# Sliding-window attention and a two-layer MLP on one core: batch 0's shifted values copied block by block, and block 0's first product taken input by input

## The chip, the cores and the metric

The kernel runs on one core of one Trainium2 chip. The metric is the device time of one execution in microseconds, lower is better. A core has five engines with queues of their own: TensorE (PE) multiplies matrices into PSUM, VectorE (DVE) and ScalarE (ACT) work on SBUF and PSUM, GpSimd (POOL) works on SBUF and issues most of this kernel's loads, SyncE (SP) issues the stores and some copies.

## The reference

```python
# q, k, v: (8, 8, 576, 64) float32; w_in: (512, 2048); w_out: (2048, 512)
scores = scale * np.matmul(q, k.transpose(0, 1, 3, 2))      # scale = 1/8
rel = pos[:, None] - pos[None, :]
mask = (rel >= 0) & (rel < 64)                               # window of 64, causal
attn = softmax(where(mask, scores, -1e9))
a = np.matmul(attn, v)                                       # (8, 8, 576, 64)
x = a.transpose(0, 2, 1, 3).reshape(4608, 512)
h = x @ w_in
g = h * np.clip(h + 3.0, 0.0, 6.0) / 6.0
out = g @ w_out                                              # (4608, 512) float32
```

## The kernel before, in words

**Work.** Attention is done in turns. A turn is one batch and one pair of heads; there are 8 batches and NG = 4 pairs, so 32 turns. A turn gives 128 rows of xT (the transposed attention output, bf16) for the 576 positions of its batch. The MLP is done in nine blocks of TB = 512 positions. A block's first product has 16 units. Unit fc multiplies the four row groups of xT (g = 0 to 3, one for each pair of heads) with w_in into one 128x512 PSUM tile hT, four matmuls in all; then ScalarE computes t1 = relu(hT/6 + 0.5) (L494) and VectorE computes gT = min(t1, 1) * hT (L495). The second product has 16 units of four matmuls each (L518), and each quarter of it ends in a ScalarE copy (L524) and a store. The order on each engine is the order of the program text: it is written out by hand, and nothing is rescheduled. Units wait in the queue `moe` until `weave(n)` takes n of them into the stream.

**Batch 0's start.** Batch 0 is treated apart. POOL issues eight loads of q and k (one for each pair of heads), the five V blocks of 128 positions (the last one 64) with `load_early_v`, three loads of w_in (columns 0 to 511, 512 to 1023, 1024 to 2047), builds the two masks with `late_windows`, and issues w_out and batch 1's loads. TensorE first multiplies zeros with `warm` as filler. Then `t_k` and `t_q` transpose keys and queries, and `s0_` computes scores and their exponentials, for each of the four turns.

**The shifted values.** A window reaches over two neighbouring stretches of 64 positions, so the product with V needs V twice: as loaded (`Vn`), and shifted by 64 positions (`Vs`). In `shift_early(g, move)` half a block of Vn goes to the other half of the partitions in Vs, for all blocks of one pair of heads: two copies for each pair, L151 (64x720) and L152 (64x576). Pairs 0 and 1 go to VectorE, 2 and 3 to ScalarE. The V part of each head is 72 columns wide, 64 values and 8 ones.

**From there to block 0.** `pv_early(t)` multiplies the exponentials with Vn and Vs for turn t: for each head of the pair, blocks m = 0 to 4 in order, two matmuls each (L354). VectorE takes the reciprocal of the sums (L363) and normalizes (L364) into `opg`. `x_early(t)` transposes opg on TensorE (L375) and ScalarE copies it to xT (L378). Then `begin(0, ...)` starts block 0: units 0 to 2 take inputs 0 to 2 (three matmuls each), x_early(3) stands between, unit 3 follows with its three, and then each of the four takes input 3 and goes on to L494. The remaining twelve units come one by one.

**PSUM.** There are eight banks: ps_t has three buffers, ps_h two, ps_acc one, and ps_o one tile of two banks. A tile can be written again once its readers are done. A unit's pool is picked by position: for block 0 `(ps_h, ps_h, ps_t, ps_acc, ps_t, ps_t)[(fc - NG) % 6]`.

**Batch 1.** Its four turns come between block 0's second-product units. The loop over turns n to n + 3 (n = 4) does `turn(t + 1)` (transposes, from the q/k loads), the scores of turn t, and then weaves 2, 4 and 2 units (L790). After the four turns come their products with V (`pv`, L403) and block 1, started by `begin(1, ...)` in the same manner as block 0.

**Loads.** POOL's issue of a load can itself wait: the semaphores of the POOL queue's loads are used in rotation, eight of them, and a load waits until the one that stood eight loads before it has landed.

Of the kernel before, what the change touches and what calls it, by code (L numbers as in the profile page):

```python
# [10 lines left out]
F32 = mybir.dt.float32  # L11
# [13 lines left out]
P = 128  # L25
D = 64
W = 64
# [9 lines left out]
def kernel(  # L37
# [9 lines left out]
    nc = tc.nc  # L47
    B, H, S, _ = q.shape
    DM, FF = moe_w_in.shape
    NT = B * S  # L50
    NG = H // 2
    SP = S // R
    NW = S // W
    NM = (S + P - 1) // P
# [89 lines left out]
            memset(t[:, :, :, 0:VO], 1.0)  # L144
            memset(t[:, :, :, VO + P : VW], 1.0)

    def shift_early(g, move):

        vn, vs = Vn[0], Vs[0]
        hs = slice(2 * g, 2 * g + 2)  # L150
        move(out=vs[W:P, :, hs], in_=vn[0:W, :, hs])  # L151
        move(out=vs[0:W, 1:NM, hs], in_=vn[W:P, 0 : NM - 1, hs])  # L152

    def shift(b):

# [4 lines left out]
    def load_w_in(i):  # L160
        n = FF // 4
        c = (slice(0, n), slice(n, 2 * n), slice(2 * n, FF))[i]
        nc.gpsimd.dma_start(
            out=win16[:, :, c], in_=moe_w_in[:, c].rearrange("(g p) f -> p g f", p=P)
        )
# [35 lines left out]
    def late_windows():  # L201

        for part in halves:
            select(band, part, -1, 1, -1, 0.0)
            select(band, part, W, -1, 1, 0.0)
            select(first, part, 0, -1, 1, 0.0)
# [29 lines left out]
    def t_k(t):  # L236
        b, g = divmod(t, NG)
        tp = transposed_heads(ps_acc, staged[b][1], g)
        nc.vector.tensor_copy(
            out=KT[t % 4][:, W:].rearrange("q (p r) -> q p r", r=R),  # L240
            in_=tp[:].rearrange("q r p -> q p r"),
        )
# [96 lines left out]
    def pv_early(t):  # L339
        b, g = divmod(t, NG)  # L340
        vn, vs, pz, pl = Vn[b % 2], Vs[b % 2], Pz[t % 4], Pl[t % 4]
        if t in (1, 3):
            os = [ps_h.tile([P, 1, 512], F32, name="oh", tag="bk") for _ in range(2)]
        else:
            os = [ps_o.tile([P, 2, 512], F32, name="o", tag="o")]
        n = len(os)
        for h in range(2):
            hh = 2 * g + h
            o = os[h % n][:, h // n]
            for m in range(NM):  # L350
                om = o[:, m * (D + 1) : (m + 1) * (D + 1)]
                for a in range(2):
                    last = m == NM - 1
                    nc.tensor.matmul(  # L354
                        om[a * W : (a + 1) * W], lhsT=pl[:, h, a * W : (a + 1) * W] if last else pz[:, h, m, a, :],
                        rhs=(vn if a and not last else vs)[:, m, hh, 0 : D + 1], start=True, stop=True,
                    )
        opg = work.tile([P, NM, 2, D], BF16, name="opg")
        for i, o in enumerate(os):
            hs = slice(i, i + 2 // n)  # L360
            ov = o[:, :, 0 : NM * (D + 1)].rearrange("p h (m c) -> p h m c", c=D + 1)
            rec = recs[:, t, hs, 0:NM]
            nc.vector.reciprocal(out=rec.unsqueeze(3), in_=ov[:, :, :, D : D + 1])  # L363
            nc.vector.tensor_tensor(  # L364
                out=opg[:, :, hs].rearrange("p m h d -> p h m d"), in0=ov[:, :, :, 0:D],
                in1=rec.unsqueeze(3).to_broadcast([P, 2 // n, NM, D]), op=MULT,
            )
        opgs[t] = opg

    def x_early(t):  # L370
        b, g = divmod(t, NG)
        opg = opgs.pop(t)
        tp = ps_t.tile([P, NM, P], BF16, name="xp", tag="bk")
        for m in range(NM):
            nc.tensor.transpose(  # L375
                out=tp[:, m, :], in_=opg[:, m].rearrange("p h d -> p (h d)"), identity=ident[:]
            )
        nc.scalar.copy(out=xT[:, g, 0:S], in_=tp[:].rearrange("p m q -> p (m q)")[:, 0:S])  # L378
# [72 lines left out]
    def x_turned(t):  # L451
        b, g = divmod(t, NG)
        opg, opg0 = opgs.pop(t)
        tp = ps_t.tile([P, S], BF16, name="xp", tag="bk")
        nc.tensor.transpose(out=tp[:, 0:W], in_=opg0[:].rearrange("p h d -> p (h d)"), identity=ident[0:D, 0:D])
        for m in range(NM - 1):
            nc.tensor.transpose(
                out=tp[:, W + m * P : W + (m + 1) * P],
                in_=opg[:, m // 2, m % 2].rearrange("p h d -> p (h d)"), identity=ident[:],
            )  # L460
        nc.scalar.copy(out=xT[:, g, b * S : b * S + S], in_=tp[:])
# [5 lines left out]
    def first_units(kb):  # L467
        t0 = kb * TB % XR
        gT = gpool.tile([P, NFC, TB], BF16, name="gT")
        gTs[kb] = gT  # L470

        def unit(fc, part=2, pool=None):
            if part < 2 and fc in halfway:
                hT = halfway.pop(fc)
            else:
                if pool is None:
                    if late[0] == 0:
                        pool = (ps_h, ps_h, ps_t, ps_acc, ps_t, ps_t)[(fc - NG) % 6]
                    else:
                        pool = ps_t if late[0] == 1 or fc % 2 else ps_h  # L480
                hT = (
                    ps_o.tile([P, 2, 512], F32, name="hTo", tag="o")[:, 0] if pool is ps_o
                    else pool.tile([P, TB], F32, name="hT", tag="bk")[:]
                )
            for g in ((0, 1, 2), (3,), range(NG))[part]:
                nc.tensor.matmul(  # L486
                    hT, lhsT=win16[:, g, fc * P : (fc + 1) * P], rhs=xT[:, g, t0 : t0 + TB],
                    start=(g == 0), stop=(g == NG - 1),
                )
            if part == 0:  # L490
                halfway[fc] = hT
                return
            t1 = t1pool.tile([P, TB], BF16, name="t1")
            nc.scalar.activation(out=t1[:], in_=hT, func=RELU, bias=half_const[:], scale=1.0 / 6.0)  # L494
            nc.vector.scalar_tensor_tensor(  # L495
                out=gT[:, fc, :], in0=t1[:], scalar=1.0, in1=hT, op0=MIN, op1=MULT
            )

        units[kb] = unit
        return [lambda fc=fc: unit(fc) for fc in range(NFC)]  # L500

    def second_units(kb):
# [32 lines left out]
    def queue_block(kb, kept=2 * NG):  # L535

        f = first_units(kb)
        moe.extend(left[:2])
        del left[:2]
        n = len(left)  # L540
        for i, unit in enumerate(f):
            moe.extend(left[i * n // NFC : (i + 1) * n // NFC])
            moe.append(unit)
        left[:] = second_units(kb)
        n = len(left) - kept
        moe.extend(left[:n])
        del left[:n]
# [3 lines left out]
        queue_block(kb, NFC)  # L551
        queue_block(kb + 1, 0)

    def begin(kb, pools, between):

        def part(fc):
            moe.popleft()
            units[kb](fc, 0, pools[fc])

        for fc in range(3):  # L560
            part(fc)
        between()
        for fc in range(3, len(pools)):
            part(fc)
        for fc in range(len(pools)):
            units[kb](fc, 1)

    def weave(n):
        for _ in range(min(n, len(moe))):
            moe.popleft()()  # L570
# [82 lines left out]

    T = B * NG

    def warm(pool, n):

        wt = pool.tile([P, TB], F32, name="wt", tag="bk")
        for _ in range(n):
            nc.tensor.matmul(wt[:], lhsT=zeros[:, 0:P], rhs=zeros[:], start=True, stop=True)  # L660

    nc.vector.memset(zeros[:], 0.0)
    nc.vector.memset(ident[:], 0.0)
# [12 lines left out]
    nc.vector.memset(first[:], 1.0)  # L676
    pads(1, nc.vector.memset)
    load_early_v()
    for i in range(3):
        load_w_in(i)  # L680
    late_windows()
    load_w_out(0)
    staged[1] = load_qk(1, 2)
# [3 lines left out]
    nc.vector.memset(recs[:], 1.0)  # L687
    zero_rows(1)
    nc.vector.memset(Pl[0][:], 1.0)
    nc.vector.memset(Vs[0][0:W, 0], 0.0)  # L690
    for t in Pl[1:]:
        nc.vector.memset(t[:], 1.0)
    nc.vector.memset(ones[:], 1.0)
# [2 lines left out]


    warm(ps_h, 12)
    t_k(0)
    t_q(0)  # L700
    t_k(1)
# [6 lines left out]
    t_k(3)  # L708
    t_q(3)
    s0_(2)  # L710
    for g in range(2):
        shift_early(g, nc.vector.tensor_copy)
    s0_(3)
    for g in range(2, NG):
        shift_early(g, nc.scalar.copy)
    warm(ps_acc, 6)
    pv_early(0)
    pv_early(1)
    warm(ps_acc, 2)
    x_early(0)  # L720
    pv_early(2)
    x_early(1)
    pv_early(3)
    x_early(2)
    queue_block(0, 0)
    begin(0, (ps_acc, ps_t, ps_t, ps_o), lambda: x_early(3))
    def group(t, n):

        if t >= 2 * NG:
# [48 lines left out]
    for t in range(n, n + 4):  # L778
        if t < n + 3:
            turn(t + 1)  # L780
        s = s_first(t, min(t + 1, n + 3))

        def copies():
            if t < n + 3:
                turned(t + 1, 0)
                turned(t + 1, 1)

        weights(t, s, s_rest(t), own, copies)
        if t < n + 3:
            weave((2, 4, 2)[t - n])  # L790
    nc.gpsimd.tensor_copy(out=seen[:], in_=P0[(n + 3) % 4][0:1, 0, 0, 0:1])
    staged[2] = load_qk(2, 1)
    for t in range(n, n + 4):
# [13 lines left out]
    late[0] = 1  # L807
    shift(2)
    queue_block(1)
    begin(1, (ps_t, ps_t, ps_acc, ps_o), lambda: x_turned(n + 3))  # L810
    pads(3, nc.gpsimd.memset)
    nc.gpsimd.tensor_copy(out=seen[:], in_=xT[0:1, NG - 1, S : S + 1])
    load_qk(2, 1, 3)
# [56 lines left out]
```

## Time and profile before

| What | Value |
|---|---|
| Median of 3 runs | 323.37 us (322.7, 323.37, 325.82) |
| Profiled execution, its own time | 324.49 us |
| Span in that profile, first to last instruction | 322.8 us |
| PE busy | 307.5 us (95% of the span) |
| DVE, ACT, POOL busy | 177.3, 187.4, 122.9 us |
| PE busy from 14 to 26 us | 10.60 of 12 us |
| PE busy from 26 to 48 us | 22.0 of 22 us |

The span is the time from the first to the last instruction in one profiled execution; the time of that execution is 1.69 us longer. A row of the profile names the source line, the engine, the operation and the tiles (output, arrow, input), the shapes and the count. "Idle before" is the time in which the engine stood still just before the row, with what ended it. Matmuls are pipelined: a row shows 379 ns for a 128x512 matmul, while one starts 0.216 us after the other.

### The profile page before, as it was taken

The numbers are of one execution on the slowest core, as the hardware profiler recorded it, in microseconds if no ns is written. First come the engines' busy times: TensorE is split into PE (matmuls) and PEld (weight loads), VectorE is DVE, ScalarE is ACT, GpSimd is POOL, SyncE is SP. The second block draws the span as 40 slices with busy tenths as digits, with TensorE's granted clock in tenths as the row PEclk, the third lists the DMA queues.
The fourth block names the chain that finished last, engine by engine and source line by source line (L and its number), as shares of the span: only waits on it lengthen the run. The fifth ranks groups of instructions, "written<-read, shape, count | busy, mean of one in ns | idle before, by whom it ended". The sixth has DMA issues, their size and how long they took to land.

```text
span 322.8 us, 11140 instructions
## 1 busy us (share of the span) xinstructions
PE 307.5 (95%) x4822; PEld 155.5 (48%) x4822; DVE 177.3 (55%) x384; ACT 187.4 (58%) x349; POOL 122.9 (38%) x167
## 2 busy tenths in 40 slices
PE   6889999999999999999999999999999999999992
PEld 2744455445444555555555555555544444444440
DVE  7676647488446752775277626762666156334300
ACT  2768565598547764776477637773674256445310
POOL 8961204688775434563356335633331000000000
PEclk9999999999999999999999999999999999999997
DMA  6999994979979942993299338943012200110011
GB/s 92 161 211 207 207 181 110 214 105 115 197 104 164 125 116 88 162 131 111 80 163 129 115 100 139 152 102 94 17 51 52 85 32 0 60 40 34 34 70 69
DMA packets 57592, 35.67 MB, mean 111 GB/s; under 512 B 39872, under 2 KB 51648, under 8 KB 57536
## 3 DMA queue, kind: packets, MB, share of 16 engines
q0 software_dynamic: 35904, 18.81, 44.6%
q1 hardware_dynamic: 21632, 16.08, 19.2%
q8 instruction: 39, 0.64, 0.8%
q14 instruction: 17, 0.14, 0.1%
HBM read 37.62 MB, written 9.44 MB: 146 GB/s over the span
## 4 chain that ended last, share of the span: by engine, by line
PE 83%; DVE 4%; DMA 3%; ACT 3%; POOL 3%; issue 2%; SPq 0%; POOLq 0%; DVEq 0%; ACTq 0%
PE hT L486 36%; PE acc L518 35%; PE o L403 4%; PE s L310 2%; PE acco L518 2%; PE tk L276 2%; DMA V<-in_v_dram 2%; DMA xT<-opg 2%; POOL qk L107 2%; POOL V L126 1%; ACT t L494 1%; DVE gT L495 1%; DVE opg L364 1%; PE tq L276 1%; ACT e L323 0%
## 5 line engine op out<-in xcount | busy, mean ns | idle before, releaser
L495 DVE SCALAR_TENSOR_TENSOR gT<-t,hT 128x512 bf16<-128x512 bf16 x142 | 97.0, 688 | 84.8 <-ACT t L494 84.0
L486 PE MATMUL hT<-xT,win 128*128 128x512 bf16 x568 | 133.9, 379 | 1.7 <-DVE gT L495 0.6
L518 PE MATMUL acc<-wout,gT 128*128 128x512 bf16 x544 | 129.0, 379 | 0.6 <-ACT QZ L283 0.6
L494 ACT ACTIVATE t<-hT,half_const 128x512 bf16<-128x512 f32 x142 | 97.0, 689 | 52.8 <-PE hT L486 52.3
L486 PEld LDWEIGHTS <-win 128*128 128x128 bf16 x576 | 55.7, 98 | 68.4 <-issue 3.4
L518 PEld LDWEIGHTS <-gT 128*128 128x128 bf16 x576 | 54.3, 98 | 63.6 <-issue 0.9
L331 POOL TENSOR_TENSOR Pz<-e,band 128x512 bf16<-128x512 bf16 x48 | 54.2, 1146 | 0.0
L328 POOL TENSOR_TENSOR P<-e,first 64x256 bf16<-64x256 bf16 x24 | 15.9, 663 | 87.4 <-ACT e L319 87.4
L524 ACT COPY osb<-acc 128x512 f32<-128x512 f32 x34 | 19.9, 586 | 42.2 <-PE acc L518 36.2
L323 ACT ACTIVATE e<-s 128x512 bf16<-128x512 f32 x56 | 30.0, 590 | 0.0
L283 DVE COPY KT<-tk 128x576 bf16<-128x576 bf16 x28 | 20.8, 743 | 5.3 <-ACT e L319 4.5
L137 POOL DMA_DIRECT2D V<-in_v_dram x22 | 18.0, 821 | 11.8 <-DMA win<-in_moe_w_in_dram 5.9
L412 DVE TENSOR_REDUCE sums<-o 128x12 f32<-128x24 f32 x26 | 4.6, 178 | 27.4 <-PE o L403 27.4
L403 PEld LDWEIGHTS <-Pz 64*64 64x64 bf16 x1120 | 13.4, 108 | 12.8 <-issue 11.4
L426 DVE TENSOR_TENSOR opl<-o,recs 128x256 bf16<-128x256 f32 x52 | 19.2, 406 | 0.0
L283 ACT COPY QZ<-tq 128x576 bf16<-128x576 bf16 x28 | 17.8, 636 | 1.5 <-PE tq L276 1.5
L319 ACT ACTIVATE e<-tk 64x128 bf16<-64x128 f32 x28 | 7.6, 271 | 14.4 <-PE tq L296 14.4
L403 PE MATMUL o<-V,Pz 64*64 64x65 bf16 x1040 | 15.3, 195 | 0.0
L310 PE MATMUL s<-QZ,KT 64*64 64x64 bf16 x896 | 14.4, 195 | 0.4 <-DVE gT L495 0.4
L276 PE MATMUL tk<-ident,qk 64*64 64x64 bf16 x504 | 14.0, 195 | 0.0
L276 PE MATMUL tq<-ident,qk 64*64 64x64 bf16 x504 | 14.0, 195 | 0.0
L276 PEld LDWEIGHTS <-qk 64*64 64x64 bf16 x1008 | 11.6, 106 | 2.3 <-issue 2.1
(102 smaller groups left out, 204.9 us busy)
## 6 DMA issues: line engine op xcount, KB each, us to landing
out_dram<-osb SPq DMA_DIRECT2D x36, 256.0 KB, 2.3
V<-in_v_dram POOLq DMA_DIRECT2D x16, 256.0 KB, 5.8
V<-V SPq DMA_DIRECT2D x6, 432.0 KB, 4.7
qk<-in_k_dram POOLq DMA_DIRECT2D x4, 576.0 KB, 5.9
qk<-in_q_dram POOLq DMA_DIRECT2D x4, 576.0 KB, 9.0
wout<-in_moe_w_out_dram POOLq DMA_DIRECT2D x2, 1024.0 KB, 19.0
qk<-in_q_dram POOLq DMA_DIRECT2D x12, 144.0 KB, 4.3
qk<-in_k_dram POOLq DMA_DIRECT2D x12, 144.0 KB, 4.3
```

The costliest lines, as they stand in the source:

```text
L276: nc.tensor.transpose(out=hosts[t][z][halves[h], r * W : (r + 1) * W], in_=staged[b][halves[z], 2 * g + h, r * D : (r + 1) * D], identity= ...
L283: (nc.scalar.copy if z else nc.vector.tensor_copy)(out=(QZ[t % 4][:, 0] if z else KT[t % 4][:, W:]).rearrange("q (p r) -> q p r", r=RL), i ...
L310: nc.tensor.matmul(ss[h][halves[i], c, m, r], lhsT=keys(t, h, W * (w - 1), r), rhs=QZ[t % 4][halves[h], 0, w * W : (w + 1) * W], start=Tru ...
L323: nc.scalar.activation(out=e[:].rearrange("p c m r w -> p (c m r w)"), in_=ss[h][:].rearrange("p c m r w -> p (c m r w)"), func=EXP, scale ...
L331: muls[h].tensor_tensor(out=Pw[t % 4][:, h].rearrange("p c m r w -> p (c m) (r w)"), in0=e[:].rearrange("p c m r w -> p (c m) (r w)"), in1 ...
L403: nc.tensor.matmul(o[i][halves[c], c0 : c0 + D + 1], lhsT=p, rhs=vt[:, 2 * g + h, v0 : v0 + D + 1], start=(r == 0), stop=(r == 1), skip_gr ...
L426: nc.vector.tensor_tensor(out=opg[:, :, i], in0=ov[i][:, 2:6, 1 : D + 1].rearrange("p (m h) d -> p m h d", h=2), in1=rec[:, i, 2:6].rearra ...
L486: nc.tensor.matmul(hT, lhsT=win16[:, g, fc * P : (fc + 1) * P], rhs=xT[:, g, t0 : t0 + TB], start=(g == 0), stop=(g == NG - 1),)
L494: nc.scalar.activation(out=t1[:], in_=hT, func=RELU, bias=half_const[:], scale=1.0 / 6.0)
L495: nc.vector.scalar_tensor_tensor(out=gT[:, fc, :], in0=t1[:], scalar=1.0, in1=hT, op0=MIN, op1=MULT)
L518: nc.tensor.matmul(acc, lhsT=gT[:, fc, ts * P : (ts + 1) * P], rhs=wout16[:, fc, :], start=(fc == 0), stop=(fc == NFC - 1),)
L524: nc.scalar.copy(out=osb[:], in_=acc)
```

## The change

Four things change, all of them before the products with V of batch 1.

- `shift_early(m, move)` now copies one block m for all eight heads, in two copies of 64x576 (the last block in one). Blocks 0 and 1 go to POOL, between the second and the third w_in load; blocks 2 to 4 go to VectorE. ScalarE has none. The memset of Vs's first rows moves ahead.
- The fillers before the first product with V are four instead of six, and four fillers of 64 columns are added after the first twelve.
- Block 0's first five units are opened together and take input 0, then 1, then 2, then 3, as x_early fills them. Units 0 to 2 are in ps_acc and two buffers of ps_t, units 3 and 4 in the two halves of one ps_o tile (`pair_bank`). `complete` adds the last input and runs the activation; for the pair, both activations follow the second unit's last matmul. Three of the four x_early tiles are now taken while two ps_t buffers are held.
- The pools of block 0's later units are picked by another rule, and the weave in batch 1 is (4, 2, 2) instead of (2, 4, 2). Block 1's start is written with the new functions; its order stays as it was.

```diff
-    def shift_early(g, move):
+    def shift_early(m, move):
 
         vn, vs = Vn[0], Vs[0]
-        hs = slice(2 * g, 2 * g + 2)
-        move(out=vs[W:P, :, hs], in_=vn[0:W, :, hs])
-        move(out=vs[0:W, 1:NM, hs], in_=vn[W:P, 0 : NM - 1, hs])
+        move(out=vs[W:P, m], in_=vn[0:W, m])
+        if m + 1 < NM:
+            move(out=vs[0:W, m + 1], in_=vn[W:P, m])
...
-                        pool = (ps_h, ps_h, ps_t, ps_acc, ps_t, ps_t)[(fc - NG) % 6]
+                        pool = ps_acc if fc == 8 else ps_h if fc in (5, 6, 11, 12) else ps_t
...
-            if part == 0:
+            if gs[-1] == NG - 1 and act:
+                hidden(fc, hT)
+            else:
                 halfway[fc] = hT
-                return
+
+        def hidden(fc, hT=None):
+            hT = halfway.pop(fc) if hT is None else hT
             t1 = t1pool.tile([P, TB], BF16, name="t1")
...
+    def pair_bank():
+        both = ps_o.tile([P, 2, 512], F32, name="hTo", tag="o")
+        return [both[:, i] for i in range(2)]
+
+    def complete(kb, fcs, pair=()):
+        unit, hidden = units[kb]
+        for fc in fcs:
+            unit(fc, (NG - 1,), act=fc not in pair)
+            if fc in pair[1:]:
+                for x in pair:
+                    hidden(x)
+        for _ in fcs:
             moe.popleft()
...
     load_early_v()
-    for i in range(3):
+    nc.vector.memset(Vs[0][0:W, 0], 0.0)
+    for i in range(2):
         load_w_in(i)
+    for m in range(2):
+        shift_early(m, nc.gpsimd.tensor_copy)
+    load_w_in(2)
     late_windows()
...
     warm(ps_h, 12)
+    warm(ps_h, 4, W)
     t_k(0)
...
-    for g in range(2):
-        shift_early(g, nc.vector.tensor_copy)
+    for m in range(2, NM):
+        shift_early(m, nc.vector.tensor_copy)
     s0_(3)
-    for g in range(2, NG):
-        shift_early(g, nc.scalar.copy)
-    warm(ps_acc, 6)
+    warm(ps_acc, 4)
     pv_early(0)
     pv_early(1)
     warm(ps_acc, 2)
     x_early(0)
     pv_early(2)
+    queue_block(0, 0)
+    u = units[0][0]
+
+    def inputs(gs, fcs, **to):
+        for fc in fcs:
+            u(fc, gs, **to)
+
+    u(0, (0,), ps_acc)
+    inputs((0,), (1, 2), pool=ps_t)
     x_early(1)
     pv_early(3)
     x_early(2)
-    queue_block(0, 0)
-    begin(0, (ps_acc, ps_t, ps_t, ps_o), lambda: x_early(3))
+    inputs((1,), range(3))
+    for fc, to in zip((3, 4), pair_bank()):
+        u(fc, (0, 1), to=to)
+    x_early(3)
+    inputs((2,), range(5))
+    complete(0, range(5), (3, 4))
...
-            weave((2, 4, 2)[t - n])
+            weave((4, 2, 2)[t - n])
...
-    begin(1, (ps_t, ps_t, ps_acc, ps_o), lambda: x_turned(n + 3))
+    u, some = units[1][0], range(NG - 1)
+    u(0, some, ps_t)
+    u(1, some, ps_t)
+    u(2, some, ps_acc)
+    x_turned(n + 3)
+    u(3, some, to=pair_bank()[0])
+    complete(1, range(4))
```

More of the change, by code (lines that the diff above doesn't have):

```diff
@@ L470, in first_units, with unit @@
         gTs[kb] = gT
-        def unit(fc, part=2, pool=None):
-            if part < 2 and fc in halfway:
+        def unit(fc, gs=range(NG), pool=None, to=None, act=True):
+            if fc in halfway:
                 hT = halfway.pop(fc)
+            elif to is not None:
+                hT = to
             else:
@@ L477, in unit @@
                     if late[0] == 0:
-                        pool = (ps_h, ps_h, ps_t, ps_acc, ps_t, ps_t)[(fc - NG) % 6]
+                        pool = ps_acc if fc == 8 else ps_h if fc in (5, 6, 11, 12) else ps_t
                     else:
                         pool = ps_t if late[0] == 1 or fc % 2 else ps_h
[L481 to L485, printed above, removed]
+                hT = pool.tile([P, TB], F32, name="hT", tag="bk")[:]
+            for g in gs:
                 nc.tensor.matmul(
@@ L497, in unit @@
             )
-        units[kb] = unit
+        units[kb] = unit, hidden
         return [lambda fc=fc: unit(fc) for fc in range(NFC)]
@@ L552, in queue_last @@
         queue_block(kb + 1, 0)
-    def begin(kb, pools, between):
-        def part(fc):
-            moe.popleft()
[L558 to L566, printed above, removed]
+    def pair_bank():
[9 more added lines that the diff above has]
+        for _ in fcs:
+            moe.popleft()
     def weave(n):
@@ L654, with warm @@
     T = B * NG
-    def warm(pool, n):
+    def warm(pool, n, cols=TB):
         wt = pool.tile([P, TB], F32, name="wt", tag="bk")
         for _ in range(n):
-            nc.tensor.matmul(wt[:], lhsT=zeros[:, 0:P], rhs=zeros[:], start=True, stop=True)
+            nc.tensor.matmul(wt[:, 0:cols], lhsT=zeros[:, 0:P], rhs=zeros[:, 0:cols], start=True, stop=True)
     nc.vector.memset(zeros[:], 0.0)
@@ L689 @@
     nc.vector.memset(Pl[0][:], 1.0)
-    nc.vector.memset(Vs[0][0:W, 0], 0.0)
     for t in Pl[1:]:
```

## The prediction

> **What bounds the kernel now.** I read the page first: busy shares and the chain that ended last.
>
> ```profile
> PE 307.5 (95%) x4822; PEld 155.5 (48%) x4822; DVE 177.3 (55%) x384; ACT 187.4 (58%) x349; POOL 122.9 (38%) x167
> ...
> PEclk9999999999999999999999999999999999999997
> ...
> PE 83%; DVE 4%; DMA 3%; ACT 3%; POOL 3%; issue 2%; SPq 0%; POOLq 0%; DVEq 0%; ACTq 0%
> ```
>
> TensorE is the bound, and its granted clock is full in every slice but the last. An edit gains only where the chain leaves PE. So I read that chain between 15 and 28 us, the stretch in which the change works:
>
> ```profile
> 10.98 5.17 DMA V<-in_v_dram
> ...
> 16.27 0.59 DVE V L151
> ...
> 17.63 0.46 DVE V L152
> ...
> 18.12 0.23 DVE recs L363
> ...
> 21.49 0.47 PE xp L375 x5
> ...
> 21.98 0.65 ACT xT L378
> ...
> 24.66 0.65 ACT xT L378
> ...
> 26.37 1.73 PE hT L486 x8
> ```
>
> The end is not set by PE here: batch 0's values land at 16.15, VectorE copies their shifted form until 18.09, then its reciprocals and products run back to back to 21.4, and two copies to xT follow. Only from 26.2 is PE fed without a gap. The table by stage shows what that leaves unused (columns: stretch; length; busy time of PE, weight loads, DVE, ACT, POOL; clock; DMA):
>
> ```profile
> 18.00:22.00 4.00, 3.30 (x77) 2.22 (x76) 3.79 (x12) 2.90 (x6) 2.69 (x4) 1.00 1.20 214
> 22.00:26.00 4.00, 3.62 (x21) 1.64 (x20) 0.65 (x3) 1.50 (x3) 0.29 (x1) 1.00 1.13 206
> 26.00:30.00 4.00, 4.00 (x20) 1.86 (x19) 3.52 (x6) 4.00 (x8) 0.88 (x1) 1.00 1.24 207
> ```
>
> The timeline of this stretch, by engine, gives the rows that are moved:
>
> ```profile
> 15.74 1.46 PE L660 MATMUL wt<-zeros 128*128 128x512 bf16 x6
> ...
> 16.66 0.79 ACT L151 COPY V<-V 64x720 bf16<-64x720 bf16 x1
> ...
> 16.88 0.31 DVE L152 COPY V<-V 64x576 bf16<-64x576 bf16 x1
> ...
> 17.63 0.46 DVE L152 COPY V<-V 64x576 bf16<-64x576 bf16 x1
> ...
> 18.98 0.67 ACT L152 COPY V<-V 64x576 bf16<-64x576 bf16 x1
> ...
> 19.75 0.64 ACT L378 COPY xT<-xp 128x576 bf16<-128x576 bf16 x1
> ...
> 26.91 0.88 POOL L137 DMA_DIRECT2D V<-in_v_dram  x1 [4.61 <-DMA win<-in_moe_w_in_dram]
> ```
>
> ScalarE's four copies end at 19.65, and x_early(0)'s copy to xT starts only then. The last row is POOL's issue of batch 1's second V load, held 4.61 us until a weight transfer had landed: transfers are queued deep here. In the built order of instructions the two kernels are alike on every engine from batch 1's last group on, so all gain or loss arises in the first 50 us.
>
> **The change part by part.**
>
> *Shift by blocks.* Gone are ScalarE's four copies, 0.79 + 0.67 + 0.79 + 0.67 = 2.92 us, and VectorE's four, 16.27 to 18.09, all of which waited for the last of five V blocks because each took a pair of heads over all blocks. New are nine copies of 64x576: four on POOL (blocks 0, 1), five on VectorE (blocks 2 to 4). The V loads are issued from 7.48 to 11.0 and land 5.2 to 5.8 us later, so blocks 0 to 4 are there at about 13.1, 13.9, 14.9, 15.8 and 16.15. VectorE is free at 14.74; its rows for this shape are 0.31 and 0.46, so blocks 2 and 3 are copied by about 16.6 and block 4 by 16.9, where before the last copy ended at 18.09.
>
> *POOL's four copies.* No row shows a POOL copy of this size. The nearest are groups of POOL by form (columns: count, busy us, mean ns, idle before):
>
> ```profile
> L331 POOL TENSOR_TENSOR Pz<-e,band 128x512 bf16<-128x512 bf16 x48 | 54.2, 1146 | 0.0
> ...
> L666 POOL TENSOR_SCALAR_AFFINE_SELECT ident<-ident 128x128 bf16<-128x128 bf16 x1 | 0.3, 309 | 0.1
> ...
> L791 POOL COPY seen<-P 1x1 bf16<-1x1 bf16 x1 | 0.2, 178 | 16.2 <-DVE P L328 16.2
> ```
>
> So: a 1x1 copy 178 ns; a select of 128x64 247 ns and of 128x128 309 ns, slope 0.97 ns an element, which gives 0.74 us at 576; the products 64x256 663 ns and 128x512 1146 ns, with two inputs, slope 1.89; half of that on top of 178 gives 0.72 us. Lower bound 0.62 (memsets: 103 ns at 1, 218 ns at 128 elements), upper bound 1.49 (2.59 ns an element, the smaller product's rate). I take 0.73, which both nearest rows give. POOL has issued the second w_in load at about 13.2, so the copies run from 13.25 to 16.2 (15.7 to 19.2 by the bounds): with 0.73, block 4 on VectorE ends last.
>
> What is queued on POOL behind them: w_in's third load, six selects for band and first, both w_out loads, four q/k loads, four V loads of batch 1. The third w_in load slides from 13.1 to 16.2 or later. The transfers are in one queue, though: the second w_in load lands at 21.15 (12.45 + 8.7), the third at 26.6 (13.1 + 13.5), so the third's bytes move only after 21.15 and an issue before about 19 costs nothing. Unit 8 is its first reader, near 28.5 in the new order. band and first are read at 42.
>
> *Fewer fillers.* Two of six fillers before the first product with V go, 2 x 0.216 = 0.43 us, PE reaches it at about 16.65 instead of 17.13. The four new 64-wide fillers stand where PE's weight loads stood idle 0.42 us for the first k load: nothing; without that cover about 0.1 us. The memset of Vs moves within a run of memsets: nothing.
>
> *First product input by input.* No matmul is added: 20 of 0.216 us for units 0 to 4. Five are now open at once, in ps_acc, two ps_t buffers and both halves of a ps_o tile. The price is that x_early(1), (2) and (3) share the third ps_t buffer: x_early(2)'s transposes wait until ScalarE has copied x_early(1)'s.
>
> *The sum.* Let R be the start of the first reciprocal (L363), 18.12 before. With the shift done at 16.9, the remaining ten matmuls of pv_early(0) put R at 17.4. By the distances of before, opg 0 to 2 are ready at R + 1.07, + 2.33 and + 3.31. Then: x_early(0) ends at 18.98; xT copy 19.0 to 19.65, no longer behind ScalarE's shift (19.75 before); three matmuls on input 0 to 20.35; x_early(1) to 20.75, its copy 20.8 to 21.45, pv_early(3) beside it; x_early(2) 21.5 to 21.95; three matmuls on input 1 to 22.55; four into the pair to 23.4; x_early(3) to 23.75, its copy 23.9 to 24.55; five on input 2 to 24.85; five on input 3 to 25.9. Unit 5 then starts at 25.9; before, unit 4's four matmuls start at 26.21 and unit 5 at 27.07. The gain is 27.07 - 25.9, about 1.1 us, and in general 18.5 - R.
>
> *Does it last?* Units 5 to 15 run on PE at 4 x 0.216 = 0.86 a unit, against 0.69 on ScalarE and on VectorE, so the five products that end together are worked off; the reassigned buffers come free in time. Later readers against landings: q/k heads for turn 6 land at 19.44 + 23.4 = 42.8; turn 6 starts at 43.2 before, and at 43.2 - 1.1 + 1.73 = 43.8 now, because the weave (4, 2, 2) puts two units of 0.86 ahead of it; without that shift 0.7 us would be lost. The same shift brings w_out's second half forward to about 42.0; it landed at 39.6. Batch 1's last V load lands at 33.66 + 14.5 = 48.2; pv of turn 4 moves from 50.97 to 49.9. So I take the whole 1.1 us. Block 1's beginning is the same order in another spelling: nothing.
>
> The profiled execution took 324.49 us (span 322.8 and 1.69 around it): 323.4 expected for it. The median, 323.37, is 1.12 lower; against it I forecast 322.3.
>
> **The rivals.**
>
> *POOL and VectorE copies take turns* instead of overlapping. For it: the one shape 64x576 took 0.31 and 0.46 us on VectorE while POOL was writing descriptors. Against: neither was held for a whole POOL instruction. Worked out: block 2's first copy waits for a POOL copy to end at 15.4, the fourth POOL copy ends at 16.4, four VectorE copies of 0.31 follow with handovers to 17.6; R = 18.05, gain 0.45: 322.9. The Trainium skill, "SBUF — State Buffer", section "Who interferes with whom", says that a VectorE copy in a two-port mode and a GpSimd instruction exclude each other for the whole instruction; by that rule this rival would be the forecast, and the trace of before has no POOL copy to decide it.
>
> *Slower: POOL's copies end last.* Mechanism: pv_early(0) needs blocks 0 and 1 from POOL; R = POOL's end + 0.6. It decides from a POOL end of 17.9, 1.17 us a copy. At the upper row, 1.49 us, POOL ends at 19.2, R = 19.8 and 1.3 us is lost: 324.6. For it: POOL's rows with two inputs are that slow. Against: a copy has one input. From an end of 20 on, w_in's third load also comes too late for its queue, and the loads behind it slip one for one; 3.2 us is lost at an end of 21.
>
> *The gain is swallowed* at the transfers of batch 1, as the slacks of 1.0 us (turn 6) and 1.7 us (last V load) are small: no change, 323.4. Against: the issue order is unchanged and DMA moved over 180 GB/s from 20 to 46 us, so landings should not move.
>
> *More than the chain shows.* The runs of before spread from 322.7 to 325.82; if that scatter arises in the start, a start with fewer waits gains up to 3 us: 320.2. No row speaks for it.
>
> **How the numbers follow.** Forecast 0.50, taking turns 0.16, slower 0.16, swallowed 0.08, more 0.10. The likeliest alone spans 321.8 to 322.8. The range takes in taking turns, swallowed and POOL's upper bound, and below the execution scatter of 0.7 under the median: 321.2 to 324.7. A measurement of this kernel tells about 1%, 3.2 us, from no change. Forecast, turns and swallowed lie within it, as does most of slower; faster by over 1% is only part of "more" (0.09), slower by over 1% is POOL ending past 21 (0.09); within 0.82.
>
> **What would show it.** Right: no ScalarE copy of V; POOL copies near 0.73 us between the second and third w_in issue; the first reciprocal near 17.4; PE without a gap from about 20 and unit 5 at 25.9; the stretch from 26 on unchanged in length; third w_in load landing at 26.6. Wrong: a POOL copy over 1.2 us, VectorE copies of block 2 held until 16, PE waiting for win at unit 8 or for qk at turn 6.

## The result, and the profile after

The changed kernel takes 322.74 us in the median of 20 runs (321.77 to 324.65). The kernel before, run beside it, takes 324.35 us (322.70 to 327.04). The ratio is 0.9951, with a 95% interval of 0.9930 to 0.9972: 1.6 us faster, between 0.9 and 2.3. A second comparison on the chip, after_again below, gave 0.9962 (0.9942 to 0.9981). The profiled execution took 323.23 us with a span of 321.5; the one before took 324.49 with 322.8.

The chain that ended last, in the stretch in which the change works, in the changed kernel (columns: start, length, what):

```profile
9.21 5.97 DMA V<-in_v_dram
...
15.62 0.67 DVE V L152
...
16.31 0.60 DVE V L150
...
17.34 0.34 DVE V L150
...
18.14 0.23 DVE recs L363
...
19.76 0.65 ACT xT L378
...
22.71 0.65 PE hT L485 x3
23.35 0.86 PE hTo L485 x4
...
26.66 1.51 PE hT L485 x7
```

The first reciprocal comes at 18.14, where before it came at 18.12: the nine copies by blocks bring it forward by nothing in this pair of executions. x_early(0)'s copy to xT stands at 19.76 (19.75 before). What differs comes after it. PE's timeline puts unit 5 at 26.49:

```profile
22.27 0.44 PE L375 MATMUL xp<-ident,opg 128*128 128x128 bf16 x5 [0.29 <-ACT xT L378]
22.54 0.81 PE L485 MATMUL hT<-xT,win 128*128 128x512 bf16 x3
23.19 1.03 PE L485 MATMUL hTo<-xT,win 128*128 128x512 bf16 x4
24.05 0.44 PE L375 MATMUL xp<-ident,opg 128*128 128x128 bf16 x5
24.33 0.81 PE L485 MATMUL hT<-xT,win 128*128 128x512 bf16 x3
24.98 0.59 PE L485 MATMUL hTo<-xT,win 128*128 128x512 bf16 x2
25.41 0.81 PE L485 MATMUL hT<-xT,win 128*128 128x512 bf16 x3
26.06 0.59 PE L485 MATMUL hTo<-xT,win 128*128 128x512 bf16 x2
26.49 7.72 PE L485 MATMUL hT<-xT,win 128*128 128x512 bf16 x35
```

The twenty matmuls of the five units are done at 26.49, 0.58 us earlier than the 27.07 of before. There, PE's rows after x_early(3) were:

```profile
24.18 0.44 PE L375 MATMUL xp<-ident,opg 128*128 128x128 bf16 x5
24.46 0.81 PE L486 MATMUL hTo<-xT,win 128*128 128x512 bf16 x3
25.35 0.81 PE L486 MATMUL hT<-xT,win 128*128 128x512 bf16 x3
26.00 0.38 PE L486 MATMUL hTo<-xT,win 128*128 128x512 bf16 x1
26.21 2.10 PE L486 MATMUL hT<-xT,win 128*128 128x512 bf16 x9
```

Before, eleven of the twenty were still to come after x_early(3) (three, three, one, and the first four of the last row), and PE stood still for 0.24 us (25.11 to 25.35) until x_early(3)'s copy had ended. In the changed kernel x_early(3) stands 0.13 earlier, at 24.05, ten are still to come, and the five on input 2 cover its copy: 0.13 + 0.22 + 0.24 is the 0.58, but for rounding.

From unit 5 to the first transposing transfer (71.82 before, 71.24 after) both kernels take 44.75 us, so nothing of the 0.58 is lost there, and the other pools of the later units cost and gain nothing. The other 0.7 us of the 1.3 us by which the spans differ arises between 71 and 126 us.

POOL's and VectorE's copies in the changed kernel show why the reciprocal did not move:

```profile
13.93 0.66 POOL L152 COPY V<-V 64x576 bf16<-64x576 bf16 x1
14.65 0.66 POOL L150 COPY V<-V 64x576 bf16<-64x576 bf16 x1
15.37 0.75 POOL L152 COPY V<-V 64x576 bf16<-64x576 bf16 x1
16.06 0.74 POOL L163 DMA_DIRECT2D win<-in_moe_w_in_dram  x1
...
15.28 0.30 DVE L150 COPY V<-V 64x576 bf16<-64x576 bf16 x1 [0.41 <-DMA V<-in_v_dram]
15.62 0.66 DVE L152 COPY V<-V 64x576 bf16<-64x576 bf16 x1
16.31 0.60 DVE L150 COPY V<-V 64x576 bf16<-64x576 bf16 x1
16.94 0.37 DVE L152 COPY V<-V 64x576 bf16<-64x576 bf16 x1
```

The VectorE copy that starts at 15.62, inside POOL's last copy, ends at 16.28, 0.16 after POOL's end at 16.12. The next one, beside POOL's issue of a load (16.06 to 16.80), ends at 16.91, 0.11 after it. Alone, this copy takes 0.30.

### The profile page after: what moved, and what is told of

Read it like the earlier page. It is cut to its first block, busy times and chain, and to the rows that moved or that the text cites. A ratio compares the mean times of both kernels' runs of the same rounds, so it can differ in the third digit from the quotient of the medians.

```text
span 321.5 us, 11140 instructions
## 1 busy us (share of the span) xinstructions
PE 307.6 (96%) x4824; PEld 156.0 (49%) x4824; DVE 177.6 (55%) x385; ACT 183.9 (57%) x345; POOL 125.3 (39%) x171
## 4 chain that ended last, share of the span: by engine, by line
PE 87%; ACT 3%; DVE 2%; POOL 2%; DMA 2%; issue 2%; POOLq 0%; ACTq 0%; DVEq 0%
PE hT L485 37%; PE acc L521 37%; PE o L403 4%; PE s L310 2%; PE acco L521 2%; DMA V<-in_v_dram 2%; PE tk L276 2%; POOL qk L107 2%; ACT t L497 1%; DVE gT L498 1%; PE tq L276 1%; POOL V L126 1%; PE hTo L485 1%; PE xp L375 0%; ACT e L323 0%
## 5 line engine op out<-in xcount | busy, mean ns | idle before, releaser
L498 DVE SCALAR_TENSOR_TENSOR gT<-t,hT 128x512 bf16<-128x512 bf16 x141 | 95.8, 687 | 82.7 <-ACT t L497 82.2
L497 ACT ACTIVATE t<-hT,half_const 128x512 bf16<-128x512 f32 x141 | 95.8, 689 | 51.1 <-PE hT L485 50.5
```

The source lines that it names most:

```text
L498: nc.vector.scalar_tensor_tensor(out=gT[:, fc, :], in0=t1[:], scalar=1.0, in1=hT, op0=MIN, op1=MULT)
```

## The experiments

Two measures from each profile carry most of the reading. R is the start of the first reciprocal; D is the time from R to the start of unit 5 (8.95 before, 8.35 in the changed kernel).

**Both kernels once more.** No edit.

> The kernel before, once more, for a second profile. Theory (gains beyond the start are scatter between executions): block 0's unit 5 starts at 27.1 again, within 0.2 us, but the three waits between 85 and 103 us (0.7 after an issue gap, 0.5 on a transposing transfer to xT, 0.6 behind a ScalarE copy to QZ) change in size or place. Rival (the later waits belong to the phase that the start sets): the same three waits in the same places, within 0.1 us each.

> The changed kernel, once more. Theory: unit 5 starts at 26.5 within 0.2 us (0.6 earlier than before), the first reciprocal at 18.1; the stretch from 85 to 103 us shows waits of another size than in its first profile; ratio about 0.997 to 0.995. Rival (phase): that stretch repeats to 0.1 us and the ratio stays at 0.995.

Measured: before_again has R = 18.08 and unit 5 at 27.03, D = 8.95. after_again has R = 18.68 and unit 5 at 27.04, D = 8.36, ratio 0.9962. So D holds to 0.01 and the gain in D is 0.60, while R went 0.54 later, because V's blocks landed later (a median of 6.1 us after their issue instead of 5.4): POOL's first copy started 0.62 later, and all of VectorE's first three copies were held. Of the three late waits of before, one was there again, larger: 1.2 us on a transposing transfer instead of 0.5. after_again had that wait too, 1.4, which the changed kernel had not shown at all. The rival, that this stretch repeats, falls for both.

**The shift alone.**

```diff
# kernel before, with
+ shift_early by blocks; blocks 0 and 1 on gpsimd ahead of load_w_in(2), 2 to 4 on vector
```

> The kernel before with the shift by blocks alone (four copies on POOL, five on VectorE, none on ScalarE); fillers, block 0's start, pools and weave as before. Theory (POOL's and VectorE's copies take turns): the first reciprocal at 18.1 as before, x_early(0)'s copy to xT at 19.75 as before, unit 5 at 27.1, ratio 1.000. Rival (the prediction's forecast, copies overlap): first reciprocal at 17.4 to 17.6, unit 5 at 26.5, ratio 0.998.

Measured: ratio 0.9996 (0.9975 to 1.0018), near the theory's 1.000, though the interval holds the rival's 0.998 too. Its profile caught an execution with late V: blocks 3 and 4 landed near 18.0, R was 19.52 and D 8.95. The absolute times expected were missed for that reason. The copies decide against the rival: VectorE's first two start inside POOL copies and end 0.17 and 0.16 us after them. D is that of before, so the shift by itself, with ScalarE free of copies, shortens nothing after the reciprocal.

**The order alone.**

```diff
# changed kernel, with the old shift (vector and scalar), load order and fillers
```

> The changed kernel with the old shift (two pairs of heads on VectorE, two on ScalarE), the old load order and the old fillers; block 0's start input by input, its pools and the weave as changed. Theory: the start's gain is the order's alone: first reciprocal 18.1, unit 5 at 26.5 to 26.6, ratio about 0.998. Rival (the order needs ScalarE free of the shift): x_early(0)'s copy is held to 19.75 and later, unit 5 at 27.0, ratio 1.000.

Measured: ratio 0.9970 (0.9947 to 0.9992). R = 18.56 and unit 5 at 27.15, so D = 8.59: 0.36 less than before, 0.24 more than in the changed kernel. The 0.24 is ScalarE, whose last shift copy ends at 20.5 and holds x_early(0)'s copy:

```profile
19.05 0.79 ACT L151 COPY V<-V 64x720 bf16<-64x720 bf16 x1
19.86 0.67 ACT L152 COPY V<-V 64x576 bf16<-64x576 bf16 x1
20.43 0.63 ACT L378 COPY xT<-xp 128x576 bf16<-128x576 bf16 x1
```

PE's wait for that copy is 0.5 here and 0.3 in the changed kernel. The scores ended late in this execution, so that ScalarE's shift began at 17.55, where it began at 16.66 before. In the profile of before the shift held nothing: x_early(0)'s copy starts 0.50 after its transposes (19.25 to 19.75), as in the changed kernel with an idle ScalarE (19.27 to 19.76), and shift_only, with ScalarE free, has the D of before. So the 0.60 in D is the order's, with the pools that it needs; the old shift takes 0.24 of it back where the scores are late. The theory is right in kind, and the rival's hold came at 0.24 us instead of the whole gain. R stood 0.50 after the last shift copy although VectorE was free: with the late scores, the six fillers kept PE from the product with V until 18.0.

**No copies on POOL.**

```diff
-    for m in range(2):
-        shift_early(m, nc.gpsimd.tensor_copy)
...
-    for m in range(2, NM):
+    for m in range(NM):
```

> The changed kernel with all nine shift copies on VectorE, none on POOL. Theory (taking turns): every copy takes 0.30 to 0.38 us, but for those beside POOL's issue of a load (up to 0.6); nine take 3.0 to 3.6 us from the time VectorE is free (about 14.9), so the last ends near 18.2 and the first reciprocal at 18.6; unit 5 8.35 us after it; ratio 0.997 to 0.998. Rival (POOL's copies cost VectorE nothing and the long copies have another cause): copies of 0.6 to 0.7 appear here as well, last copy at 19.5 or later, ratio above 0.999.

Measured: ratio 0.9976 (0.9954 to 0.9997). Eight of nine VectorE copies take 0.30 to 0.32; one, at 16.18, takes 0.74:

```profile
15.91 0.91 POOL L169 DMA_DIRECT2D wout<-in_moe_w_out_dram  x1
16.81 0.65 POOL L118 DMA_DIRECT2D qk<-in_k_dram  x1
...
16.18 0.74 DVE L152 COPY V<-V 64x576 bf16<-64x576 bf16 x1
16.95 0.30 DVE L150 COPY V<-V 64x576 bf16<-64x576 bf16 x1
```

The long one stands beside POOL's issue of a w_out load and ends 0.10 us after it; the next, beside the issue of a k load, takes 0.30. Nothing of 0.66 to 0.69 is left, so the long copies of the changed kernel are POOL's doing. R = 18.40, D = 8.35: R lies between the two of the changed kernel, 18.14 and 18.68, so handing two blocks to POOL shows neither a clear gain nor a clear loss.

**The copies in 32-bit words.**

```diff
-        move(out=vs[W:P, m], in_=vn[0:W, m])
+        move(out=vs[W:P, m].bitcast(F32), in_=vn[0:W, m].bitcast(F32))
... (and the second copy likewise)
```

> The changed kernel with the nine shift copies made on 32-bit words (64x288 float32 instead of 64x576 bf16), the same bytes. Theory (a VectorE copy can't run beside a POOL copy, it ends 0.16 to 0.17 us after it): POOL's four copies shrink from 0.66 to 0.4 to 0.5 us each and end 0.7 to 1.0 us earlier, so that at most one or two VectorE copies are held; the last of the five VectorE copies ends within 1.9 us of the first one's start (2.4 to 2.8 us in the changed kernel), and the first reciprocal comes 0.3 to 0.6 us earlier against the landing of block 2. Ratio to before 0.994. Rival (the landing of V alone sets the first reciprocal): nothing moves, ratio as the changed kernel's, 0.996.

Measured: ratio 0.9953 (0.9929 to 0.9978). POOL's copies take 0.42 instead of 0.66, and only VectorE's second one is held long, beside POOL's issue of the third w_in load:

```profile
14.94 0.42 POOL L152 COPY V<-V 64x288 f32<-64x288 f32 x1
15.31 0.74 POOL L163 DMA_DIRECT2D win<-in_moe_w_in_dram  x1
...
15.15 0.38 DVE L150 COPY V<-V 64x288 f32<-64x288 f32 x1 [0.26 <-DMA V<-in_v_dram]
15.56 0.60 DVE L152 COPY V<-V 64x288 f32<-64x288 f32 x1
16.19 0.37 DVE L150 COPY V<-V 64x288 f32<-64x288 f32 x1
```

It ends at 16.16, 0.11 after that issue. R = 17.73 and unit 5 at 26.08, the earliest so far. From the start of the first VectorE copy to the end of the last it is 2.10 us, against 2.39 and 2.79 in the two profiles of the changed kernel; 1.9 was expected. The rival falls by R; the ratio's interval can't tell this version from the changed kernel.

**The same, with the selects ahead of the third w_in load.**

```diff
-    load_w_in(2)
     late_windows()
+    load_w_in(2)
```

> The kernel with 32-bit shift copies, and the six selects for the two masks ahead of the third w_in load. Theory: the second VectorE copy stands beside a POOL select (0.3 to 0.4 us) and not beside the issue of a load (0.60), so the last copy ends 0.2 us earlier against block 2's landing; the third w_in load is issued near 17.3, before the second has landed, and costs nothing; ratio to before 0.994 to 0.995. Rival: the late issue shows, PE waits for win at unit 8, ratio 0.996 or more.

Measured: ratio 0.9947 (0.9915 to 0.9978). No VectorE copy is longer than 0.41; the five take 1.94 us from first start to last end; R = 17.69, unit 5 at 26.05. The third w_in load is issued at 17.32 and lands at 26.8, and PE waits for no weights. The profiles put this version and the one before 0.4 us ahead of the changed kernel's first profile; the times alone do not show it.

**The old weave, and the new weave alone.**

```diff
# weave_old: changed kernel with    # weave_only: kernel before with
-            weave((4, 2, 2)[t - n])     -            weave((2, 4, 2)[t - n])
+            weave((2, 4, 2)[t - n])     +            weave((4, 2, 2)[t - n])
```

> The changed kernel with the weave of before in batch 1, (2, 4, 2). Theory: turn 6 comes 1.73 us earlier, near 41.8 to 42.6 us, and PE waits there for a load of q or k that lands near 42.8: a wait of 0.3 to 1.0 us, ratio 0.998 to 0.999. Rival (the loads are there in time): no such wait, ratio 0.996.

> The kernel before with the new weave (4, 2, 2) alone. Theory: unit 5 at 27.1 and the first transposing transfer 44.75 us after it, as in every run so far; no stall at turn 6; ratio 1.000, within 0.002. Rival (the new weave eases a later stretch: over the profiles so far, from the first transposing transfer at about 71 us to the ninth, kernels with the old weave took 53.8 to 54.4 us and those with the new one 52.6 to 54.7): that stretch takes 53.4 us or less and the ratio is 0.998.

Measured: weave_old has a ratio of 0.9969 (0.9944 to 0.9993); turn 6's first transpose of k starts at 42.59, and its first transpose of q only at 42.76, since q's load lands at 42.72: a wait of 0.17 us. From unit 5 to the first transposing transfer it is 44.92 us instead of 44.75; but pool_none, with the new weave and no such wait, has 44.95, so it is the wait and not this distance that shows the 0.17. The theory is right in kind, and its 0.3 to 1.0 was too much. weave_only has 0.9989 (0.9963 to 1.0016), with unit 5 at 27.1; a gap of 0.6 us that no semaphore explains put its first transfer 45.5 us after unit 5 instead of 44.75, which the expectation missed (the ten profiles ahead of it had 44.74 to 44.95). From that transfer to the ninth it took 53.65 us. So the weave's effect is 0.17 us at turn 6, which is below what either ratio can tell; that of weave_only lies between its theory and its rival.

**The old fillers.**

```diff
-    warm(ps_acc, 4)
+    warm(ps_acc, 6)
```

(The four 64-column fillers go as well.)

> The changed kernel with the fillers of before: six instead of four ahead of the first product with V, none of 64 columns. Theory: PE reaches the first product with V 0.43 us later, but waits there less for VectorE's copy of block 4 (0.54 in the changed kernel), so the first reciprocal comes within 0.46 us of that copy's end as before, unit 5 8.35 us after the reciprocal, clock 1.00 in every stretch: ratio 0.996, as the changed kernel. Rival (the fillers are on the path): the reciprocal comes 0.4 us later against the copy, ratio 0.997 to 0.998.

Measured: ratio 0.9972 (0.9951 to 0.9993). The last VectorE copy ends at 17.94 and R is 18.49: 0.55 between them, where the changed kernel has 0.47. D = 8.36. In this execution the scores ended late, so 0.08 us of the fillers lay on the path. Both expectations are half right: two fillers cost nothing when V is late, and something when the scores are; 0.08 us is measured, and 0.43 (2 x 0.216) is an estimate of the most, which order_only, with 0.50 between its last copy and R, would have come near.

**V's last block late.** In both kernels its load is moved behind the first w_in load.

```diff
# both: load_early_v for blocks 0 to 3, then
+    load_w_in(0)
+    load_early_v((NM - 1,))
+    load_w_in(1)
```

> The kernel before with the load of V's last block moved behind the first w_in load, so that it lands about 2.4 us later, near 18.6. Theory (the old shift waits for all of V, the new one only for each block): all four VectorE copies wait for it, first reciprocal 1.9 us after the landing, near 20.5, 2.4 us later than before; ratio to before 1.006 to 1.008. Rival (lateness of V is no part of it): first reciprocal moves less than 1 us, ratio 1.002 or less.

> The changed kernel with the same late load of V's last block. Theory: only the fifth VectorE copy waits; first reciprocal 0.9 us after the landing, near 19.5, 1.3 us later than in the changed kernel; unit 5 8.35 us after the reciprocal; ratio to before 1.000 to 1.001, so 1.6 to 1.7 us better than the kernel before with the same late load (0.6 us from the order, 1.0 from the shift). Rival: the two kernels with late V differ by 0.6 us only, as with V in time.

Measured: the block landed at 19.48 in the kernel before (11.76 + 7.72) and at 18.94 in the changed one (11.69 + 7.25). R followed 1.64 us later in the kernel before, with all four VectorE copies behind the landing, and 0.79 later in the changed one, with one copy behind it: the mechanism of the theory, at 0.85 us instead of 1.0. The ratios are 1.0076 (1.0044 to 1.0108), as expected, and 1.0037 (1.0008 to 1.0066), above the expected 1.001. They differ by 0.0039, 1.3 us, where 1.6 to 1.7 was expected and the rival said 0.6; the two intervals overlap, so the times do not decide. In the profiles the lead at unit 5, counted from the landing, is 0.8 us (10.60 against 9.82), nearer to the rival. What is missing can be seen: D was 9.03 in after_late_v instead of 8.35. The table by stage of after_late_v says why (the clock is the third column from the right):

```profile
18.00:20.00 2.00, 0.69 (x32) 0.69 (x31) 0.54 (x3) 0.00 (x0) 1.87 (x6) 0.92 1.26 208
20.00:23.00 3.00, 2.93 (x33) 1.65 (x31) 2.57 (x7) 0.64 (x1) 3.00 (x5) 0.50 1.14 217
23.00:26.00 3.00, 2.56 (x37) 1.72 (x37) 1.74 (x5) 1.28 (x2) 1.14 (x2) 0.98 1.14 203
```

and PE's timeline of it:

```profile
17.27 0.22 PE L354 MATMUL o<-V,Pz 128*64 128x65 bf16 x2 [0.18 <-DVE V L150]
19.31 0.22 PE L354 MATMUL o<-V,Pl 128*64 128x65 bf16 x2 [1.82 <-DVE V L150]
...
20.08 1.03 PE L663 MATMUL wt<-zeros 128*128 128x512 bf16 x2
20.91 0.74 PE L375 MATMUL xp<-ident,opg 128*128 128x128 bf16 x5
```

After 1.82 us without work PE's granted clock was 0.50 for some 3 us: two fillers took 1.03 us instead of 0.60, five transposes 0.74 instead of 0.45. These lie on the path to unit 5, and D is 0.68 us longer than in the changed kernel. Without that the lead would have been near 1.5, an estimate from 0.8 and 0.68.

## Why the prediction was right or wrong

**The time and the sign** were right: 322.3 forecast, 322.74 measured, within 321.2 to 324.7. Of the gain, 1.1 us was forecast and 1.6 measured, with 1.1 inside the interval of 0.9 to 2.3. That the time came so near is in part luck: the kernel before took 324.35 us beside it, not the 323.37 from which the forecast started, and the start gave 0.6 us, half of what was forecast. The rest is no term of the sum.

**R, the first reciprocal: wrong.** The sum put it at 17.4, and 0.72 of the 1.1 us on that. It was 18.14, 0.02 later than before. The failing step is the one that let VectorE's copies of blocks 2 and 3 run beside POOL's (0.31 and 0.46 each): the last copy ended at 17.67 instead of 16.9, and with 0.30 for each of the five and 0.03 between them it would have ended at 16.9, an estimate from the start of the first at 15.28. Its rival, taking turns, gave R = 18.05 and a gain of 0.45, and the profile shows 18.14 and 0.58: for R, that rival was the case, and the gain of the start is the order's. Three runs show the mechanism: pool_none loses the long copies, words shortens them with POOL's, words_selects removes the one beside the load's issue. The Trainium skill, "SBUF — State Buffer", section "Who interferes with whom", has this rule, and the trace agrees, with the 0.16 above (0.16 or 0.17 in all ten shift copies that start at least 0.2 us before the end of one of POOL's).

**POOL's copies: right.** 0.73 us forecast, 0.66 measured (0.75 where VectorE's held it); the end at 16.12 against 16.2. The third w_in load was issued at 16.06 and landed at 26.3 (26.6 forecast): the loads behind it were issued up to 3 us later and landed no later (w_out's second half at 39.5 against 39.6), and the slower case did not come.

**From R to unit 5: right in form, too long by 0.15.** The sum gave 8.5, the profiles 8.35 or 8.36 in seven of them. Against the 8.95 of before, the sum laid 0.45 us to this part, and 0.60 was measured: by shift_only, order_only, weave_old and fillers_old it is the order's. ScalarE's shift did not hold x_early(0)'s copy in the profile of before, as the prediction read it; it does so only where the scores are late (0.24 in order_only). x_early(2)'s wait for the shared ps_t buffer was 0.29, as the sum allowed.

**Edits put at nothing.** The two fillers less were worth 0.08 us in one execution with late scores (fillers_old), at most 0.43 by the estimate above. The weave was said to save 0.7 us at turn 6; weave_old shows 0.17. With the start 0.6 instead of 1.1 us earlier, turn 6 came there at 42.6, just ahead of its load's landing at 42.7: the term was right in kind and mis-sized.

**Swallowed: did not come.** 44.75 us from unit 5 to the first transposing transfer in both kernels.

**The rest of the gain** is not settled. The start accounts for 0.6 us in the profiles; the medians of the two comparisons differ by 1.6 and 1.0, and order_only, with a ratio of 0.9970, can't be told from the changed kernel by its times. Two things are shown to add in some executions: V's last block late (after_late_v against before_late_v), and scores late (the fillers). How often they do is not known. The stretch from 71 to 126 us differs by up to 2 us between executions of these kernels (52.6 to 54.7 without late V), through waits at transposing transfers and gaps in issue, which can make up much of the scatter of the runs; that the change eases it is neither shown nor excluded. The prediction's rival "more than the chain shows" pointed at scatter in the start, and has that much truth.

## What to carry to other kernels

Split a copy by when its data lands, and not by heads, where the last piece can be late: that was worth 0.85 us at R with the last block late, and nothing with it in time. If the halves go to GpSimd and VectorE at once, count bf16 copies there as taking turns; packing them into 32-bit words cut GpSimd's from 0.66 to 0.42 us. Order a product by when its inputs become ready: 0.6 us came from the same matmuls in another order. When a stage's start jitters by half a microsecond from one execution to the next, compare distances inside a profile (here R to unit 5, stable to 0.01 in seven profiles), not times from its start.

## What the runs showed of the hardware that was not expected

POOL's issue of a weight load holds a VectorE copy as POOL's own copy does: 0.60 instead of 0.30, ending 0.11 us after the issue, in the changed kernel and in words, and gone in words_selects. Not every issue does: beside those of q and k loads, three copies in pool_none took 0.30 each. Why they differ is open.

In after_late_v TensorE's granted clock fell to 0.50 for some 3 us after a gap of 1.82 us, while a gap of 1.79 us in before_late_v left it alone (two fillers in 0.60 us afterwards). What stands before the gaps differs: two short matmuls after a further wait of 0.18 us in the first, fillers in a row in the second. Whether that decided, one execution of each can't tell. The Trainium skill, "TensorE: Matmul & The Clock Gate", section "What's actually happening", speaks of about 3.4 us idle before the clock halves, counted in a window that runs freely; the length of the slow stretch fits that window, the gap ahead of it was shorter.
